# Where the products with v stand in the step of an attention kernel, and GpSimd's subtraction in four parts

## The chip, the cores and the metric

The kernel runs on one core of a Trainium2 chip. The metric is the device time of one execution in microseconds (us); three executions of the kernel before are known, and one more that was recorded by the hardware profiler. The engines are written as the profile writes them: PE is TensorE (PEld its weight loads), DVE VectorE, ACT ScalarE, POOL GpSimd, and SP the engine whose queue issues most of the DMAs.

## The reference, cut to what matters

Attention with a learned position bias for 4 batches and 8 heads, 576 positions and 64 channels, and behind it a feed-forward layer on the 2304 tokens:

```python
scores = scale * np.matmul(q, k.transpose(0, 1, 3, 2))
psi_rel = np.log1p(np.abs(pos[:, None] - pos[None, :]))
psi_i = np.log1p(np.maximum(pos[:, None], 1.0))
h = np.maximum((psi_rel / psi_i)[..., None] @ w1 + b1, 0.0)
scores = scores + (h @ w2).transpose(2, 0, 1)[None]
attn = np.exp(scores - np.max(scores, axis=-1, keepdims=True))
attn = attn / (np.sum(attn, axis=-1, keepdims=True) + 1e-09)
x = np.matmul(attn, v).transpose(0, 2, 1, 3).reshape(2304, 512)
h = x @ w_in
sp = np.where(h > 20.0, h, np.log1p(np.exp(np.minimum(h, 20.0))))
out = (h * np.tanh(sp)) @ w_out
```

The weights of the layer come as 64-bit floats.

## The kernel before, in words

The program has three stages: the position bias is computed and written to DRAM (to about 57 us of the profile), then the attention (to about 358 us), then the feed-forward layer. The change touches the attention alone.

**Pairs and steps.** The 32 products of batch and head are worked on as 16 pairs of heads (`i`, four pairs of heads `hp` with four batches `b` each). A pair has five steps, in the order 0, 1, 4, 2, 3 of its row chunks `c`; their places are `x` = 0 to 4, and steps are numbered `n` = 5i + x. The order of instructions on every engine is the order in which the code is written (there is no scheduler), and each engine works in order. One call of `step(n)` writes:

- `scores(n)` (L218): 16 matmuls of 128x288 columns into two units of PSUM (`s`; two buffers). The row of q is multiplied as a rounded part (`qkhi`) and a remainder (`qlo`). Then `add_bias` on DVE (L234), which writes `pt` and the row's maximum `m`, and `exps(n, 0)` on ACT (L249).
- `transposes(n - 2)`: PE turns the exponentials of the step before the last one, 128x128 at a time (L283, L286; for chunk 4 L296, L300), and ACT copies them to `main` and `tail` (L284, L290, L297, L301). PSUM has three buffers `tp` for it. The reciprocals' turn at x = 1 (L289) goes through a copy on DVE (`rt`, L264).
- `exps(n, 1)`, `ahead(n)` with the loads to come, and `split(n)` with pieces of work for later.
- `pv_duo`: the products with v. Chunks 0 and 1 of a pair form group 0, chunks 4, 2 and 3 group 1. A group has five products (`k` = 0 to 4) of two heads, that share 128x64 halves of the array, and gather in one PSUM tile `o`, of which there is one buffer. When k = 4 is done, DVE copies it to `x` (L327) and SP stores that to DRAM.

A group's five products are spread over steps: group 0 at x = 4 (two), x = 0 (two) and x = 1 (one), group 1 at x = 2 (three) and x = 3 (two).

**What comes ahead.** At x = 0 of pair i `ahead` issues the loads for pair i + 1: `qkhi` (1216 KB, L170) on POOL's queue, and `rawqk` (two halves of 304 KB, L161 and L162) and v on SP's. There are two buffers of `qkhi` and one of `rawqk`. `split` has POOL compute the remainders: `split_k` (L175) and `split_q` (L180) subtract the rounded values from the raw ones, 64x1216 elements each. They run for pair i + 1 while PE is on pair i; `rawqk` comes free when split_q has read it. In every fourth pair SP's queue also carries the bias of the next two heads, 2.6 MB in pieces, ahead of the next `rawqk`. SP's queue carries the weights of the layer too (L105), which DVE turns into 32-bit floats in pieces during all steps: L119, L122, L124 and L126, 32 weight tiles of 128x512.

For chunk 4, `exps` ends with a small copy inside `pt` on POOL (128x64, L252), which the transposes of chunk 4 need.

Of the kernel before, what the change touches and what calls it, by code (L numbers as in the profile page):

```python
# [7 lines left out]
F32 = mybir.dt.float32  # L8
# [3 lines left out]
ALU = mybir.AluOpType  # L12
# [3 lines left out]
B, H, S, D, C = 4, 8, 576, 64, 32  # L16
# [5 lines left out]
QW = 1216  # L22
# [24 lines left out]
def kernel(ctx: ExitStack, tc, qk, v, wb, w2, w_in, w_out, psia, psi4, rinv, eye, out):  # L47
    nc = tc.nc
    pe, dve, act, pool, sp = nc.tensor, nc.vector, nc.scalar, nc.gpsimd, nc.sync
# [58 lines left out]
    def conv_weights(on_act):  # L108

        job, w = w64.pop(0)
        late = order.index(job) >= EARLY
        c = (ring if late else convp).tile([P, 512], F32, name="w32")
        cu = c.bitcast(U32)
        if on_act:
            act.mul(c, w.bitcast(F32)[:, :, 1], 2.0 ** -112)
        else:
            dve.tensor_scalar(c, w.bitcast(F32)[:, :, 1], 2.0 ** -112, None, op0=ALU.mult)  # L119

        def parts():
            dve.tensor_scalar(w[:, :, 0], w[:, :, 0], 29, None, op0=ALU.logical_shift_right)  # L122
            yield False
            dve.scalar_tensor_tensor(cu, cu, 3, w[:, :, 0], op0=ALU.logical_shift_left, op1=ALU.bitwise_or)  # L124
            yield False
            dve.scalar_tensor_tensor(cu, w[:, :, 1], 0x80000000, cu, op0=ALU.bitwise_and, op1=ALU.bitwise_or)  # L126
            w32.append((job, c))
            yield True
        return parts()
# [23 lines left out]
    qk_raw, qk_hi, q_lo, v_t, bias_t = {}, {}, {}, {}, {}  # L153
# [16 lines left out]
        pool.dma_start(out=hi, in_=qk[b, hp])  # L170
        qk_hi[i] = hi

    def split_k(i):
        kl = qk_hi[i][64:128, QW:]
        (pool if i else dve).tensor_tensor(kl, qk_raw[i][64:128], kl.bitcast(F32), op=ALU.subtract)  # L175

    def split_q(i):

        lo = q_los[i % 2]
        (pool if i else dve).tensor_tensor(lo[0:64], qk_raw.pop(i)[0:64], qk_hi[i][0:64, :QW].bitcast(F32), op=ALU.subtract)  # L180
        q_lo[i] = lo

    def load_bias(hp, c):
# [12 lines left out]
    NPAIR = B * HP  # L196
    steps = [(i, c) for i in range(NPAIR) for c in ORDER]
    NS = len(steps)
    pt_t, live, o_t, sums, rc = {}, {}, {}, {}, {}
# [39 lines left out]
    def exps(n, u):  # L239

        i, c = steps[n]
        if u == 1 and c == 4:
            return
        if i not in sums:
            sums[i] = st.tile([P, 9], F32, name="sums", bufs=3)
        pt, m = live[n]
        ps = pt[:, u * S:(u + 1) * S]
        k = 4 * u + c if c < 4 else 8
        act.activation(ps, ps, AF.Exp, bias=m[:, u:u + 1], scale=-1.0, accum_out=sums[i][:, k:k + 1])  # L249
        if c == 4:  # L250

            pool.tensor_copy(pt[:, S:640], pt[:, 512:S])  # L252

    def reciprocals(i):

# [5 lines left out]
    def store_reciprocals(i, r, tp):  # L261
        hp, b = divmod(i, B)
        rt = xs.tile([9, P], F32, name="rt", bufs=1)
        dve.tensor_copy(rt, tp[0:9, P:2 * P])  # L264
        sp.dma_start(out=r_d[b][hp], in_=rt)

    def transposes(n):
        i, c = steps[n]
        pt, m = live.pop(n)
        grp = 0 if c < 2 else 1  # L270
        if (i, grp) not in pt_t:
            w = 256 if grp == 0 else 320
            main = ptp.tile([P, 2, 4, w], F32, name=f"main{grp}")
            tail = ptp.tile([P, 256 if grp == 0 else 384], F32, name=f"tail{grp}")
            pt_t[i, grp] = (main, tail)
        main, tail = pt_t[i, grp]
        if c < 4:
            off = c * P if grp == 0 else 64 + (c - 2) * P
            for h in range(2):
                tp = t_ps.tile([P, 512], F32, name="tp")  # L280
                for k in range(4):
                    c0 = h * 640 + k * P
                    pe.transpose(tp[:, k * P:(k + 1) * P], pt[:, c0:c0 + P], ident)  # L283
                act.copy(main[:, h, :, off:off + P], tp.rearrange("p (k q) -> p k q", k=4))  # L284
            tp = t_ps.tile([P, 512], F32, name="tp")
            pe.transpose(tp[:, :P], pt[:, 512:640], ident)  # L286
            r = rc.pop(n, None)
            if r is not None:
                pe.transpose(tp[0:9, P:2 * P], r, ident)  # L289
            act.copy(tail[:, off:off + P], tp[:, :P])  # L290
            if r is not None:
                store_reciprocals(i, r, tp)
        else:
            tp = t_ps.tile([P, 512], F32, name="tp")
            for k in range(4):
                pe.transpose(tp[:, k * P:(k + 1) * P], pt[:, k * P:(k + 1) * P], ident)  # L296
            act.copy(main[:, :, :, 0:64].rearrange("p h k q -> p k h q"),  # L297
                     tp.rearrange("p (k h q) -> p k h q", k=4, h=2))
            tp = t_ps.tile([P, 512], F32, name="tp")
            pe.transpose(tp[:, :P], pt[:, 512:640], ident)  # L300
            act.copy(tail[:, 0:64], tp[:, 0:64])  # L301
            act.copy(tail[:, 320:384], tp[:, 64:128])

    def pv_duo(i, grp, k):
        hp, b = divmod(i, B)
        main, tail = pt_t[i, grp]
        vt = v_t[i]
        w = 256 if grp == 0 else 320
        if k == 0:
            o_t[0] = o_ps.tile([P, 512], F32, name="o")  # L310
        o = o_t[0]
        kw = dict(skip_group_check=True)
        if k < 4:
            for h in range(2):
                pe.matmul(o[h * 64:h * 64 + 64, :w], vt[:, h, k, :], main[:, h, k, :],  # L315
                          start=(k == 0), stop=False, **kw)
            return
        if grp == 0:
            for h in range(2):
                pe.matmul(o[h * 64:h * 64 + 64, :w], vt[:, h, 4, :], tail, start=False, stop=True, **kw)  # L320
        else:
            pe.matmul(o[0:64, :w], vt[:, 0, 4, :], tail[:, 0:320], start=False, stop=True, **kw)
            pe.matmul(o[64:128, 64:320], vt[:, 1, 4, :], tail[:, 64:320], start=False, stop=True, **kw)
            pe.matmul(o[64:128, 0:64], vt[:, 1, 4, :], tail[:, 320:384], start=False, stop=True, **kw)
        del pt_t[i, grp]
        x = xs.tile([P, 320], F32, name="x")
        dve.tensor_copy(x[:, :w], o[:, :w])  # L327
        if grp == 0:
            sp.dma_start(out=x_d[b][:, hp, 0:256], in_=x[:, :256])
        else:  # L330
            sp.dma_start(out=x_d[b][:, hp, 256:512], in_=x[:, 64:320])
            sp.dma_start(out=x_d[b][:, hp, 512:576], in_=x[:, 0:64])

    LAG = 2
# [47 lines left out]
    def split(n):  # L382

        i, x = divmod(n, 5)
        if (x == 1 or n == 3) and i + 1 < NPAIR:
            split_k(i + 1)
        if x == 3 and i + 1 < NPAIR:
            split_q(i + 1)

        for _ in range((2, 2, 2, 1, 2)[x]):  # L390
            if not conv and w64:
                conv.append(conv_weights(x == 2))
            elif conv and next(conv[0]):
                conv.clear()
                load_weights()
                if w32[0][0] in order[:EARLY]:
                    split_weights(pool)

    def step(n):
        i, x = divmod(n, 5)  # L400
        late = n == 4

        def begin():
            if n < NS:
                scores(n)
                add_bias(n)
                exps(n, 0)

        def end():
            if n < NS:  # L410
                exps(n, 1)
                ahead(n)
            if 0 <= n - 1 < NS and (n - 1) % 5 == 4:
                rc[n - 1] = reciprocals((n - 1) // 5)
            if n < NS:
                split(n)


        if not late:
            begin()  # L420
        for k in {3: (0, 1)}.get(n, (n - LAG,)):
            if 0 <= k < NS:
                transposes(k)
        if not late:
            end()

        if late:
            for k in range(5):
                pv_duo(0, 0, k)
        for j, grp, ks in {4: ((i, 0, (0, 1)),), 0: ((i - 1, 0, (2, 3)),), 1: ((i - 1, 0, (4,)),),  # L430
                           2: ((i - 1, 1, (0, 1, 2)),), 3: ((i - 1, 1, (3, 4)),)}[x]:
            if 0 <= j < NPAIR and (j, grp) != (0, 0):
                for k in ks:
                    pv_duo(j, grp, k)
        if late:
            begin()
            end()

# [34 lines left out]
    for idx, t in enumerate(ts):  # L475
        spent["a"] += 1.0 + (1.9 if idx in SOFT_AT else 0.0)
        spent["v"] += (1.7 if idx in SOFT_AT else 0.0) + (1.4 if idx in (9, 12) else 0.0)
        n = reach(t)[2]
# [36 lines left out]
    for idx in range(NB + 2):  # L515
        if idx < NB:
            t = ts[idx]
            make_h(idx + 2)
            n = reach(t)[2]
# [32 lines left out]
    for n in range(len(SOFT_AT), NS):  # L552
        step(n)
# [103 lines left out]
    hidden(*units[0])  # L657
    step(NS + 1)
    step(NS + 2)
    step(NS + 3)  # L660
    left_scope.close()

    wq = sbuf("wq")
# [82 lines left out]
```

## Time and profile before

| | |
|---|---|
| median of three executions | 769.67 us (769.43 to 774.86) |
| profiled execution, its own time | 776.47 us |
| its span, first to last instruction | 774.7 us |
| attention stage within it | about 57 to 358 us |
| granted clock of PE, mean | 0.977 |

The profiled execution is 6.8 us above the median and 1.6 us above the highest of the three. All rows below come from it. A row of a timeline has the start in us from the span's start, the busy time in us, the engine, the line, the operation, what is written and read, the shape and the count; a bracket at its end gives the engine's idle time before it and what ended that.

### The profile page before, as it was taken

How to read it: one execution, taken by the hardware profiler on the slowest of the kernel's cores; microseconds unless marked ns; L12 is line 12 of the kernel's file. 1: busy time of each engine (PE TensorE's matmuls, PEld its weight loads, DVE VectorE, ACT ScalarE, POOL GpSimd, SP SyncE). 2: the span in 40 equal slices, each digit the busy share in tenths (PEclk: the TensorE clock that was granted, in tenths of full speed). 3: DMA queues.
4: the chain of work that ended last, by engine and by line, in shares of the span. 5: the costliest groups of instructions: out<-in, count | busy, mean ns of one | idle time of the engine just before them, and what ended most of it. 6: DMA issues, size and time to landing. Idle time of an engine off the chain costs nothing.

```text
span 774.7 us, 11579 instructions
## 1 busy us (share of the span) xinstructions
PE 723.3 (93%) x4160; PEld 553.0 (71%) x4160; DVE 525.1 (68%) x1047; ACT 459.5 (59%) x982; POOL 110.9 (14%) x76
## 2 busy tenths in 40 slices
PE   6688989899988998979999999999999999999997
PEld 3226667676766676756888888888987888888886
DVE  7974788678857876744977856656557566665554
ACT  6986777677756776746766644444444554444443
POOL 1003443333332334350000000000000000000000
PEclk9989999999989999989999999999999999999999
DMA  8988469876975697820400003000410500010001
GB/s 280 297 282 278 121 207 316 211 238 189 320 213 165 200 320 227 252 52 16 117 1 2 0 20 90 0 1 1 129 35 1 136 0 1 1 55 1 1 0 55
DMA packets 45610, 93.60 MB, mean 121 GB/s; under 512 B 13408, under 2 KB 22256, under 8 KB 43504
## 3 DMA queue, kind: packets, MB, share of 16 engines
q1 hardware_dynamic: 42672, 72.70, 32.0%
q0 software_dynamic: 2304, 19.92, 7.8%
q8 instruction: 33, 0.54, 0.3%
q10 hardware_dynamic: 576, 0.22, 0.1%
q14 instruction: 25, 0.20, 0.1%
HBM read 72.43 MB, written 20.40 MB: 120 GB/s over the span
## 4 chain that ended last, share of the span: by engine, by line
PE 57%; DMA 16%; DVE 8%; ACT 5%; POOL 3%; issue 2%; SPq 2%; DVEq 0%; POOLq 0%; ACTq 0%
PE y L631 24%; PE h L593 24%; DMA rawqk<-in_qk_dram 4%; PE s L218 3%; PE o L315 3%; DMA bias<-bias_d 3%; DMA w<-in_w_out_dram 3%; DVE pt L234 2%; PE tp L283 2%; POOL qkhi L175 1%; ACT pt L249 1%; DMA w<-in_w_in_dram 1%; DMA vt<-in_v_dram 1%; ACT main L284 1%; DMA qkhi<-in_qk_dram 1%
## 5 line engine op out<-in xcount | busy, mean ns | idle before, releaser
L249 ACT ACTIVATE pt<-pt,m 128x576 f32<-128x576 f32 x144 | 112.8, 784 | 90.5 <-DVE m L234 90.5
L234 DVE CUSTOM_DVE_ANT_0 pt<-s,bias 128x576 f32<-128x576 f32 x144 | 103.8, 752 | 38.9 <-PE s L218 38.1
L631 PE MATMUL y<-who,ghi 128*128 128x512 f32 x288 | 113.8, 395 | 0.2 <-ACT ghi L615 0.2
L631 PE MATMUL y<-who,glo 128*128 128x512 f32 x288 | 113.9, 396 | 0.0
L631 PE MATMUL y<-wlo,ghi 128*128 128x512 f32 x288 | 113.7, 395 | 0.0
L615 ACT CAST ghi<-e 128x512 fp32r<-128x512 f32 x72 | 44.7, 621 | 89.9 <-DVE e L611 89.8
L315 PE MATMUL o<-main,vt 128*64 128x320 f32 (+1 forms) x512 | 79.8, 436 | 8.1 <-DVE x L327 8.0
L598 ACT ACTIVATE e<-h 128x512 f32<-128x512 f32 x72 | 42.9, 598 | 71.4 <-PE h L593 71.4
L218 PE MATMUL s<-qkhi 128*128 128x288 f32 x320 | 79.2, 330 | 3.9 <-issue 2.7
L599 DVE TENSOR_SCALAR e<-e 128x512 f32<-128x512 f32 x72 | 30.7, 426 | 76.2 <-ACT e L598 76.2
L593 PE MATMUL h<-xhi,whi 128*128 128x512 f32 (+1 forms) x320 | 81.0, 373 | 0.8 <-ACT xhi L575 0.7
L593 PE MATMUL h<-xlo,whi 128*128 128x512 f32 (+1 forms) x320 | 80.4, 372 | 0.9 <-DVE xlo L577 0.8
L593 PE MATMUL h<-xhi,wli 128*128 128x512 f32 (+1 forms) x320 | 80.0, 371 | 0.0
L616 DVE TENSOR_TENSOR glo<-e,ghi 128x512 fp32r<-128x512 f32 x72 | 49.7, 690 | 43.8 <-ACT ghi L615 43.8
L218 PE MATMUL s<-qkhi,qlo 128*128 128x288 f32 x320 | 71.0, 304 | 6.3 <-POOL qlo L180 6.3
L218 PEld LDWEIGHTS s<-qkhi 128*128 128x128 f32 x320 | 51.5, 195 | 32.5 <-issue 22.0
L283 PE MATMUL tp<-ident,pt 128*128 128x128 f32 x512 | 69.6, 281 | 1.0 <-ACT main L284 0.9
L284 ACT COPY main<-tp 128x512 f32<-128x512 f32 x128 | 67.7, 578 | 0.7 <-PE tp L283 0.5
L593 PEld LDWEIGHTS h<-xhi,whi 128*128 128x128 f32 x320 | 57.2, 188 | 14.1 <-ACT xhi L575 2.1
L593 PEld LDWEIGHTS h<-xlo,whi 128*128 128x128 f32 x320 | 56.8, 188 | 12.9 <-DVE xlo L577 1.7
L593 PEld LDWEIGHTS h<-xhi,wli 128*128 128x128 f32 x320 | 56.8, 188 | 11.3
L631 PEld LDWEIGHTS y<-who,glo 128*128 128x128 f32 x288 | 54.1, 188 | 13.7 <-DVE glo L616 0.9
(75 smaller groups left out, 1160.6 us busy)
## 6 DMA issues: line engine op xcount, KB each, us to landing
qkhi<-in_qk_dram POOLq DMA_DIRECT2D x16, 1216.0 KB, 7.7
bias_d<-bt SPq DMA_DIRECT2D x36, 295.5 KB
rawqk<-in_qk_dram SPq DMA_DIRECT2D x32, 304.0 KB
w<-in_w_in_dram SPq DMA_DIRECT2D x16, 512.0 KB
w<-in_w_out_dram SPq DMA_DIRECT2D x16, 512.0 KB
vt<-in_v_dram SPq DMA_DIRECT2D x16, 320.0 KB
bias<-bias_d SPq DMA_DIRECT2D x16, 288.0 KB
out_dram<-w SPq DMA_DIRECT2D x17, 256.0 KB
```

What stands on the lines that cost most here:

```text
L218: pe.matmul(s[:, j, :SH], stat[:, q0:q0 + P], hi[:, QW + kc + j * SH:QW + kc + (j + 1) * SH], start=(k == 0), stop=(k == len(todo) - 1))
L234: dve.tensor_tensor_reduce(out=halves(pt[:, sl]), in0=s[:, :, :SH], in1=halves(bt[:, sl]), scale=-0.125, scalar=BIG, op0=ALU.add, op1=ALU. ...
L249: act.activation(ps, ps, AF.Exp, bias=m[:, u:u + 1], scale=-1.0, accum_out=sums[i][:, k:k + 1])
L283: pe.transpose(tp[:, k * P:(k + 1) * P], pt[:, c0:c0 + P], ident)
L284: act.copy(main[:, h, :, off:off + P], tp.rearrange("p (k q) -> p k q", k=4))
L315: pe.matmul(o[h * 64:h * 64 + 64, :w], vt[:, h, k, :], main[:, h, k, :], start=(k == 0), stop=False, **kw)
L593: pe.matmul(h[:, u * n:(u + 1) * n], w["i", g4, d][:, r * P:(r + 1) * P], x[:, d, :n], start=(k == 0), stop=(k == 11))
L598: act.activation(e, h, AF.Exp)
L599: dve.tensor_scalar(e, e, E20, None, op0=ALU.min)
L615: act.copy(ghi, e)
L616: dve.tensor_tensor(glo, e, ghi.bitcast(F32), op=ALU.subtract)
L631: pe.matmul(ys[blk][t], g[:, c0:c0 + P], w, start=(f == 0 and k == 0), stop=(f == NFC - 1 and k == 2))
```

## The change

The five products of a group are issued in one step: group 0 at x = 4, group 1 at x = 2 of the next pair. They stand between the step's scores and its transposes (n = 4 keeps an order of its own). The copy of `o` and the store of `x` come at the end of the same step. `split_k` and `split_q` of pairs 1 to 15 are written as four subtractions of 64x304 each; those of K in steps x = 1 and 2, those of q in x = 3 and 4 (for pair 1 all eight at n = 3). The small copy for chunk 4 goes from POOL to ACT.

```diff
+    QPART = QW // 4
+    def split_k(i, parts=range(4)):
+        for r in parts if i else (slice(0, QW),):
+            r = r if i == 0 else slice(r * QPART, (r + 1) * QPART)
+            kl = qk_hi[i][64:128, QW:][:, r]
+            (pool if i else dve).tensor_tensor(kl, qk_raw[i][64:128, r], kl.bitcast(F32), op=ALU.subtract)
...
-            pool.tensor_copy(pt[:, S:640], pt[:, 512:S])
+            act.copy(pt[:, S:640], pt[:, 512:S])
...
         del pt_t[i, grp]
+
+    def store_x(i, grp):
...
-        if (x == 1 or n == 3) and i + 1 < NPAIR:
-            split_k(i + 1)
-        if x == 3 and i + 1 < NPAIR:
-            split_q(i + 1)
+        if i + 1 < NPAIR:
+            if n == 3:
+                split_k(1)
+                split_q(1)
+            elif i and x == 1:
+                split_k(i + 1, (0, 1))
...
+        pv = [(j, grp) for at_x, j, grp in ((4, i, 0), (2, i - 1, 1)) if x == at_x and 0 <= j < NPAIR]
...
+        if late:
+            turn()
+            products()
+        begin()
         if not late:
-            begin()
-        for k in {3: (0, 1)}.get(n, (n - LAG,)):
-            if 0 <= k < NS:
-                transposes(k)
-        if not late:
-            end()
...
+            products()
+            turn()
+        end()
+        for j, grp in pv:
+            store_x(j, grp)
...
-    step(NS + 3)
```

On PE before, from the end of the scores at x = 4 of a pair over x = 0 of the next (`main_1096` belongs to group 0; the count is of k and heads):

```order
L218 MATMUL s<-qkhi,qlo_117 128x288 x2
L296 MATMUL tp<-ident,pt_1092 128x128 x4
L300 MATMUL tp<-ident,pt_1092 128x128
L315 MATMUL o<-main_1096,vt 64x256 x4
L218 MATMUL s<-qkhi 128x288 x2
L218 MATMUL s<-qkhi,qlo_116 128x288 x2
L218 MATMUL s<-qkhi 128x288 x2
L218 MATMUL s<-qkhi,qlo_116 128x288 x2
L283 MATMUL tp<-ident,pt 128x128 x8
L286 MATMUL tp<-ident,pt 128x128
L315 MATMUL o<-main_1096,vt 64x256 x4
L218 MATMUL s<-qkhi 128x288 x2
```

Two products stand behind the transposes of either step. The same place now:

```order
L225 MATMUL s<-qkhi,qlo_117 128x288 x2
L322 MATMUL o<-main_1115,vt 64x256 x8
L327 MATMUL o<-tail_1116,vt 64x256 x2
L303 MATMUL tp<-ident,pt_1099 128x128 x4
L307 MATMUL tp<-ident,pt_1099 128x128
L225 MATMUL s<-qkhi 128x288 x2
L225 MATMUL s<-qkhi,qlo_116 128x288 x2
L225 MATMUL s<-qkhi 128x288 x2
L225 MATMUL s<-qkhi,qlo_116 128x288 x2
L290 MATMUL tp<-ident,pt 128x128 x8
L293 MATMUL tp<-ident,pt 128x128
L225 MATMUL s<-qkhi 128x288 x2
```

All ten have moved between the scores and the transposes of x = 4, and x = 0 holds scores and transposes alone.

On POOL before, one round for a pair (K, the small copy, q, the next load):

```order
L175 TENSOR_TENSOR qkhi<-rawqk,qkhi 64x1216
L252 COPY pt_1535<-pt_1535 128x64
L180 TENSOR_TENSOR qlo_116<-rawqk,qkhi 64x1216
L170 DMA qkhi<-in_qk_dram 128x2432
L175 TENSOR_TENSOR qkhi<-rawqk,qkhi 64x1216
```

And now:

```order
L180 TENSOR_TENSOR qkhi<-rawqk,qkhi 64x304 x4
L187 TENSOR_TENSOR qlo_116<-rawqk,qkhi 64x304 x4
L170 DMA qkhi<-in_qk_dram 128x2432
L180 TENSOR_TENSOR qkhi<-rawqk,qkhi 64x304 x4
L187 TENSOR_TENSOR qlo_117<-rawqk,qkhi 64x304 x4
```

Nothing stands between K and q any more, and each is four instructions.

On SP before, ahead of the load of `rawqk`, from x = 3 of a pair to x = 0 of the next:

```order
L331 DMA x_d_80<-x 128x256
L332 DMA x_d_80<-x 128x64
L105 DMA w_2077<-in_w_in_dram 128x1024
L161 DMA rawqk<-in_qk_dram 64x1216
L162 DMA rawqk<-in_qk_dram 64x1216
```

And now, from x = 2:

```order
L343 DMA x_d_81<-x 128x256
L344 DMA x_d_81<-x 128x64
L105 DMA w_2342<-in_w_in_dram 128x1024
L341 DMA x_d_82<-x 128x256
L161 DMA rawqk<-in_qk_dram 64x1216
L162 DMA rawqk<-in_qk_dram 64x1216
```

The store of group 0 has come to stand right before the load of `rawqk`; it stood at x = 1 of the next pair, behind it.

## Rows read from the trace of the kernel before

**Rows 1.** Whom PE waited for from 56 to 358 us: us in total, times, longest us.

```profile
PE tp L300 <- POOL pt L252: 8.8, 5, 3.2
PE o L315 <- DVE x L327: 7.1, 10, 2.7
PE s L218 <- POOL qlo L180: 6.3, 5, 3.8
...
PE s L218 <- DVE m L234: 1.3, 2, 0.9
PE tp L283 <- ACT main L284: 0.9, 2, 0.6
```

**Rows 2.** PE's timeline: a step without products (from 74.03 us) and one with a group's last product (from 94.89 us).

```profile
74.03 0.51 PE L218 MATMUL s<-qkhi 128*128 128x288 f32 x2
...
75.17 1.03 PE L283 MATMUL tp<-ident,pt 128*128 128x128 f32 x8
...
76.18 0.51 PE L218 MATMUL s<-qkhi 128*128 128x288 f32 x2
...
94.89 1.04 PE L283 MATMUL tp<-ident,pt 128*128 128x128 f32 x8
...
96.08 0.65 PE L320 MATMUL o<-tail,vt 128*64 128x256 f32 x4
96.66 0.53 PE L218 MATMUL s<-qkhi 128*128 128x288 f32 x2
```

**Rows 3.** PE's timeline over one pair, from x = 0 to the next x = 0: its first scores, products of eight matmuls and the scores behind them, the only wait in the pair, the next pair's first scores.

```profile
243.31 0.53 PE L218 MATMUL s<-qkhi 128*128 128x288 f32 x2
...
245.54 1.08 PE L315 MATMUL o<-main,vt 128*64 128x256 f32 x8
246.56 0.53 PE L218 MATMUL s<-qkhi 128*128 128x288 f32 x2
...
252.27 1.83 PE L315 MATMUL o<-main,vt 128*64 128x320 f32 x12 [0.48 <-DVE x L327]
...
260.32 0.53 PE L218 MATMUL s<-qkhi 128*128 128x288 f32 x2
```

**Rows 4.** The timeline of all engines at 231 us, where POOL and DVE meet.

```profile
231.24 0.41 DVE L122 TENSOR_SCALAR w<-w 128x512 uint32<-128x512 uint32 x1
...
231.56 2.74 POOL L175 TENSOR_TENSOR qkhi<-rawqk,qkhi 64x1216 fp32r<-64x1216 f32 x1 [9.28 <-DMA rawqk<-in_qk_dram]
...
231.69 3.17 DVE L124 SCALAR_TENSOR_TENSOR w<-w,w 128x512 uint32<-128x512 uint32 x1
...
235.24 1.84 PE L315 MATMUL o<-main,vt 128*64 128x320 f32 x12 [2.69 <-DVE x L327]
...
235.79 0.68 DVE L126 SCALAR_TENSOR_TENSOR w<-w,w 128x512 uint32<-128x512 uint32 x1
```

**Rows 5.** DVE's groups by shape from 58 to 358 us: count, busy us, mean ns of one, idle us before them.

```profile
L126 DVE SCALAR_TENSOR_TENSOR w<-w,w 128x512 uint32<-128x512 uint32 x32 | 28.7, 896 | 0.5
L124 DVE SCALAR_TENSOR_TENSOR w<-w,w 128x512 uint32<-128x512 uint32 x32 | 28.6, 895 | 0.5
L122 DVE TENSOR_SCALAR w<-w 128x512 uint32<-128x512 uint32 x32 | 24.2, 755 | 0.8 <-DMA w<-in_w_out_dram 0.8
```

**Rows 6.** POOL's timeline: ends of two rounds of K, small copy and q, the begin of the next round, and two products of 128x512 back to back.

```profile
219.00 2.76 POOL L180 TENSOR_TENSOR qlo<-rawqk,qkhi 64x1216 fp32r<-64x1216 f32 x1
...
236.90 0.24 POOL L252 COPY pt<-pt 128x64 f32<-128x64 f32 x1 [2.59 <-ACT pt L249]
...
257.64 0.59 POOL L252 COPY pt<-pt 128x64 f32<-128x64 f32 x1
258.19 2.79 POOL L180 TENSOR_TENSOR qlo<-rawqk,qkhi 64x1216 fp32r<-64x1216 f32 x1
...
271.66 2.79 POOL L175 TENSOR_TENSOR qkhi<-rawqk,qkhi 64x1216 fp32r<-64x1216 f32 x1 [10.17 <-DMA rawqk<-in_qk_dram]
...
339.62 2.49 POOL L380 TENSOR_TENSOR xraw<-xraw,xr 128x512 f32<-128x512 f32 x2 [2.46 <-DMA xr<-r_d]
```

**Rows 7.** The timeline of all engines in the pair behind a load of bias: the load of `rawqk` leaves SP's queue, K's subtraction begins, PE waits for the small copy behind it.

```profile
129.55 0.57 SPq L161 DMA_DIRECT2D rawqk<-in_qk_dram  x1
...
141.72 2.75 POOL L175 TENSOR_TENSOR qkhi<-rawqk,qkhi 64x1216 fp32r<-64x1216 f32 x1 [13.55 <-DMA rawqk<-in_qk_dram]
...
144.91 0.33 PE L300 MATMUL tp<-ident,pt 128*128 128x128 f32 x1 [2.05 <-POOL pt L252]
```

**Rows 8.** The timeline of all engines at x = 1 of the pair of rows 3 (its scores on PE begin at 246.56 us).

```profile
247.39 0.76 DVE L234 CUSTOM_DVE_ANT_0 pt<-s,bias 128x576 f32<-128x576 f32 x1 [0.86 <-PE s L218]
...
248.25 0.77 ACT L249 ACTIVATE pt<-pt,m 128x576 f32<-128x576 f32 x1 [0.49 <-DVE m L234]
...
249.02 1.05 ACT L284 COPY main<-tp 128x512 f32<-128x512 f32 x2
...
249.96 0.28 ACT L290 COPY tail<-tp 128x128 f32<-128x128 f32 x1
```

**Rows 9.** The stretches of the attention in which PE's clock was granted at half (the second of six, and the sum of all): us, busy us and counts by engine, granted clock, DMA share, GB/s.

```profile
83.82:87.24 3.42, 3.42 (x15) 2.31 (x16) 0.73 (x3) 3.42 (x10) 2.36 (x2) 0.50 0.49 156
...
sum 27.31, PE 25.50 PEld 18.73 DVE 18.76 ACT 18.33 POOL 13.51; mean PE 4.25 PEld 3.12 DVE 3.13 ACT 3.06 POOL 2.25
```

**Rows 10.** DVE's waits from 26 to 60 us, the end of the bias stage: us in total, times, longest us.

```profile
DVE pt L234 <- PE s L218: 5.2, 1, 5.2
```

More of the change, by code (lines that the diff above doesn't have):

```diff
@@ L171, in load_hi, with split_q @@
         qk_hi[i] = hi
[L173 to L177, printed above, removed]
+    QPART = QW // 4
[4 more added lines that the diff above has]
+            (pool if i else dve).tensor_tensor(kl, qk_raw[i][64:128, r], kl.bitcast(F32), op=ALU.subtract)
+    def split_q(i, parts=range(4)):
         lo = q_los[i % 2]
-        (pool if i else dve).tensor_tensor(lo[0:64], qk_raw.pop(i)[0:64], qk_hi[i][0:64, :QW].bitcast(F32), op=ALU.subtract)
+        for r in parts if i else (slice(0, QW),):
+            r = r if i == 0 else slice(r * QPART, (r + 1) * QPART)
+            (pool if i else dve).tensor_tensor(lo[0:64, r], qk_raw[i][0:64, r], qk_hi[i][0:64, r].bitcast(F32), op=ALU.subtract)
         q_lo[i] = lo
@@ L325, in pv_duo @@
         del pt_t[i, grp]
+    def store_x(i, grp):
+        hp, b = divmod(i, B)
+        w = 256 if grp == 0 else 320
+        o = o_t[0]
         x = xs.tile([P, 320], F32, name="x")
@@ L384, in split @@
         i, x = divmod(n, 5)
-        if (x == 1 or n == 3) and i + 1 < NPAIR:
-            split_k(i + 1)
-        if x == 3 and i + 1 < NPAIR:
-            split_q(i + 1)
+        if i + 1 < NPAIR:
[4 more added lines that the diff above has]
+                split_k(i + 1, (0, 1))
+            elif i and x == 2:
+                split_k(i + 1, (2, 3))
+            elif i and x >= 3:
+                split_q(i + 1, ((0, 1), (2, 3))[x - 3])
         for _ in range((2, 2, 2, 1, 2)[x]):
@@ L416, in end, with products, turn @@
                 split(n)
-        if not late:
-            begin()
-        for k in {3: (0, 1)}.get(n, (n - LAG,)):
-            if 0 <= k < NS:
-                transposes(k)
-        if not late:
-            end()
[L427 to L437, printed above, removed]
+        pv = [(j, grp) for at_x, j, grp in ((4, i, 0), (2, i - 1, 1)) if x == at_x and 0 <= j < NPAIR]
+        def products():
+            for j, grp in pv:
+                for k in range(5):
+                    pv_duo(j, grp, k)
+        def turn():
+            for k in {3: (0, 1)}.get(n, (n - LAG,)):
+                if 0 <= k < NS:
+                    transposes(k)
+        if late:
+            turn()
+            products()
+        begin()
+        if not late:
+            products()
+            turn()
+        end()
+        for j, grp in pv:
+            store_x(j, grp)
     bc = bsbuf("bc")
```

## Prediction

> **What bounds the kernel now.** I read the waits of PE first. From 56 to 358 us PE is what the attention is made of, and three entries hold nearly all its losses: 8.8 us for POOL's small copy, 7.1 us for DVE's copy of `o`, 6.3 us for the remainder of q [rows 1]. What is to be seen is that none of the three is work of PE: each is a place where another engine, in its own order, stands behind something else.
>
> Then one quiet pair, to see PE's own price. From 243.31 to 260.32 us it takes 17.01 us, of which 0.48 is the wait for `o` [rows 3]. So 16.53 us are PE's work and what its changes of kind cost.
>
> Then the steps. A step without products takes 75.17 - 74.03 = 1.14 us of scores and 76.18 - 75.17 = 1.01 us of ten transposes. One with a group's last product takes 96.66 - 94.89 = 1.77 us from the transposes to the next scores [rows 2]. Eight product matmuls take 246.56 - 245.54 = 1.02 us [rows 3], four take 96.66 - 96.08 = 0.58 [rows 2], so one is 0.11 us and four are 0.44. The rest, 1.77 - 1.01 - 0.44 = 0.32 us, is what one visit to the products costs, whatever is done in it.
>
> Then DVE and POOL. At 231.69 us an L124 that should take about 0.68 us (L126 beside it, of the same kind, does) takes 3.17: it ends 0.56 us after POOL's K subtraction does. The copy of `o` stands behind it, and PE waits 2.69 us [rows 4]. Against 0.68 and 0.41 us unhindered [rows 4], the groups of DVE lose 32 x (0.896 - 0.68) = 6.9 us in L126, 6.9 in L124 and 32 x (0.755 - 0.41) = 11.0 in L122 [rows 5]: some 25 us of DVE's time, mostly hidden.
>
> Last, the loop that runs beside PE: q subtracted, `rawqk` free, the next load, K subtracted, q subtracted. From the end of q's subtraction to the begin of the next K it takes 231.56 - 221.76 = 9.8 us [rows 4, 6] or 271.66 - 260.98 = 10.7 us [rows 6]. With two subtractions of 2.76 and a copy this makes some 16.5 us, as long as PE's pair. Where bias was loaded it is longer: the load leaves SP at 129.55 us and K begins at 141.72 [rows 7]. There PE waits, whatever it does before.
>
> **The change, part by part.** *Visits to the products* fall from five to two a pair: 3 x 0.32 = 0.96 us less. This counts where PE sets the pace. Of the pairs 2 to 14 I leave out the bias pairs 3, 7 and 11 and the ones behind them, 4, 8 and 12, paced by DMA, and count pair 1: 8 pairs, -7.7 us. The price is measured for transposes to products to scores; the new order is scores to products to transposes. Bounds: nothing saved, or 0.96 in all 14, -13.4.
>
> *The wait for `o`.* The copy of `o` now has two or three steps of time before the next group needs the buffer, where it had none. The 7.1 us go: -7.1. At either end this is the surest term.
>
> *What is late next there.* The products now stand right behind the scores, so they need ACT's copies of the step before sooner. In rows 8, from the begin of the scores at 246.56 [rows 3], the first bias add comes at +0.83, the exponential at +1.69, the two `main` copies from +2.46 to +3.51, `tail` until +3.68. With no products in between PE would be there after 1.14 + 1.01 + 1.14 = 3.29 us [rows 2]. So PE waits 0.22 us at least at x = 4. At x = 2 it is more: two light steps come in a row, and the 0.86 us that DVE had idle before this add [rows 8] vanish with the 1.02 us of products of the step before. I take 0.5 there, 0.7 a pair, 8 pairs: +5.6. Bounds: 0, and 1.5 us a pair, where all of ACT's lateness falls on PE.
>
> *POOL's parts.* 64x1216 takes 2.74 us [rows 4], 128x512 2.49 / 2 = 1.25 back to back [rows 6]. The line through both has 0.16 us at zero columns and 2.1 ns a column, so 64x304 should take 0.80 us. Eight are 6.4 us against 2 x 2.76 plus a copy of 0.24 to 0.59 [rows 6], 5.8 to 6.1. The loop would then be 9.8 to 10.7 + 6.4 = 16.2 to 17.1 us. PE would like 17.01 - 0.48 - 0.96 + 0.7 = 16.27 us. The loop's middle, 16.65, is 0.4 above that: +3.2 in 8 pairs. Bounds: 0, and the third rival.
>
> *What the parts give.* Scores of x = 0 need q in pieces: the first unit its first quarter, the second its third. So the first unit can go 5 x 0.80 = 4.0 us after K begins, the second 7 x 0.80 = 5.6; before, both stood until about 5.9 (141.72 to 2.76 behind the copy's end at 144.86) [rows 7]. PE gains between 0.3 and 1.9 us in each place where it waits for `rawqk`. I take 1 in the three pairs behind a bias load, and 1 in the last, where the longest wait of 3.8 us is [rows 1]: -4.0.
>
> *DVE's losses.* A DVE operation can now be held for the rest of one part, 0.8 us, not 2.74. Most of the 25 us were hidden; what shows besides `o` is PE's 1.3 and 0.9 us behind `m` and ACT's copies [rows 1], of which I take 1.5: -1.5. The clock was at half from 83.82 to 87.24 us behind these two waits; if they go, 3.42 / 2 = 1.7 us go with it [rows 9]: -1.7.
> The row shows an operation of DVE held until POOL's whole instruction was over. The Trainium skill, SBUF — State Buffer, "Who interferes with whom", says that DVE and GpSimd share a pair of ports as an exclusive lock, which whoever starts first keeps for the whole instruction. By it four parts cut the hold to one part, as summed; but it works both ways, and each part can lose the lock to DVE, which is the third rival.
>
> *The small copy.* On POOL it stood behind K's subtraction, which waits for DMA; on ACT it stands behind the exponential that it needs. Of the five waits, two of about 0.66 us go: -1.3. The other three (2.05 us in rows 7, up to 3.2 in rows 1; 7.5 together) come in the pairs behind bias loads, where K begins late: PE runs on and meets the same delay at x = 0. I take nothing; bound: all 7.5. On ACT the copy costs 16 times about 0.25 us, hidden in its idle time (0.49 us before one exponential, rows 8); without that cover 4 us.
>
> *The store of x* now stands ahead of `rawqk`'s load on SP, and with it the wait for the products of x = 4 and DVE's copy. That copy follows the same pieces of conversion that held the weights' load ahead of `rawqk` before. I take 0; bound 0.8 us a pair (a copy and an issue), in the pairs that the loop sets, which is inside the loop's bounds.
>
> *The start and the end.* For pair 1 POOL no longer waits for the small copy, so its eight parts run in the bias stage and hold DVE there by up to 6.4 us. DVE finishes that stage 5.2 us early [rows 10]: +1.0. The drain has two visits fewer: -0.6.
>
> **The sum.** -7.7 - 7.1 + 5.6 + 3.2 - 4.0 - 1.5 - 1.7 - 1.3 + 1.0 - 0.6 = -14.1 us. The profiled execution would come to 776.5 - 14.1 = 762.4 us. It lies 6.8 us above the median of 769.67, and some of its waits may be missing in the others; I take the same 14.1 us off the median: **755.6 us**.
>
> **The rivals.** *1: the DMA pairs recover too.* If `rawqk` lands earlier because everything ahead of it on SP does, the 7.5 us of waits for the small copy go, and so does half of the half-clock time behind them, (27.31 - 3.42) / 4 = 6.0 us [rows 9]. For it: SP's bias loads are issued as DVE frees the tiles, so they follow PE's pace. Against: 12 us from issue to K is a queue of bytes, not of waits. 755.6 - 13.5 = 742 us.
>
> *2: the new wait eats the visits.* If PE waits 1.44 us a pair for ACT's copies, the sum of 0.96 and the old 0.48, the pair is as long as before: +5.9, and with nothing gained behind bias loads (+3) the time is 764.5 us. For it: PE's two light steps of 2.15 us each meet an ACT that needs 3.68 us from scores to `tail`. Against: the heavy steps let DVE and ACT catch up.
>
> *3: POOL's loop becomes the bound, and the kernel slower.* The place is POOL between K's first part and q's last. Each part that meets a conversion piece on DVE waits for it, 0.41 to 0.69 us. If four of eight do, the loop is 16.65 + 2.2 = 18.85 us: +2.2 in 8 pairs and in 3 behind bias loads, 24 us: 780 us. It decides from a round of 7.2 us on, 0.9 a part, where the loop passes the 17.0 us of today's pair. For it: the small copy took 0.59 us instead of 0.24 once [rows 6], so POOL is held too. Against: 2.74 to 2.80 for whole subtractions shows that it is seldom.
>
> *4: the parts don't do what they should.* If POOL goes from part to part with DVE still held, DVE loses up to 2.7 us as before, now behind `m`; without -3.2 and with one wait of 2 us more: 761 us. No row shows two POOL instructions with a DVE operation held between them.
>
> **How the numbers follow.** Forecast 0.46, rival 1 0.14, rival 2 0.20, rival 3 0.10, rival 4 0.10. One per cent of the median, 7.7 us, is about what the three runs can tell from no change: they reach 0.7% apart. Below 762.0 us lie the forecast, rival 1 and two thirds of rival 4: 0.67. Above 777.4 lies rival 3: 0.10. The rest, 0.23, is within. The range takes in rivals 2 and 4, the forecast with its bounds (the wait for ACT from 0 to 1.5 us a pair, visits up to -13.4) and all but the end of rival 1: 742 to 772 us.
>
> **What would show it.** PE's waits for the small copy and for `x` should be gone, those for `qlo` larger in the three pairs behind bias loads, and a new one for ACT's `main` should stand before the products, under 1 us. A part should take 0.8 us, a round of eight 6.4 to 7. No conversion piece on DVE should take over 1.6 us. A quiet pair should take 16.3 to 16.7 us. The forecast is wrong if a part takes over 0.9 us, or if the wait before the products passes 1.4 us.

## The result and the profile after

The changed kernel takes 782.38 us (781.1 to 783.32) against 772.22 of the kernel before (769.43 to 774.86): a ratio of 1.0114, with an interval from 1.0072 to 1.0157. The forecast was 755.6 us, faster by 1.8%; the measured time is 10.2 us above the kernel before and 10 us above the range. The profiled execution takes 782.27 us (span 780.1), 5.8 us more than the profiled one of before; that one lies 4.3 us above its median, so the profiles show little more than half of the loss.

Whom PE waits for in the changed kernel from 56 to 362 us (us in total, times, longest; answers to [rows 1]):

```profile
PE s L225 <- POOL qlo L187: 12.9, 16, 1.4
PE o L322 <- ACT main L291: 7.4, 7, 3.7
PE s L225 <- issue: 3.9, 1, 3.9
PE s L225 <- DVE m L241: 2.8, 6, 1.0
PE s L225 <- POOL qkhi L180: 2.4, 3, 1.6
```

The waits for the small copy and for `x`, 15.9 us before, are gone, as forecast. PE now waits for POOL's parts, 19 times in 15 pairs.

A quiet pair on PE (answers to [rows 3]): first scores, the first of two visits to products, the next pair's first scores.

```profile
247.13 0.51 PE L225 MATMUL s<-qkhi 128*128 128x288 f32 x2
...
252.82 2.58 PE L322 MATMUL o<-main,vt 128*64 128x320 f32 x15 [0.21 <-ACT main L291]
...
263.43 0.51 PE L225 MATMUL s<-qkhi 128*128 128x288 f32 x2
```

It takes 16.30 us, where 16.27 was forecast. What PE does by itself became shorter, though by less than was forecast (see below). The other side is POOL. Its groups from 58 to 358 us, and then DVE's conversions (answers to [rows 5]):

```profile
L187 POOL TENSOR_TENSOR qlo<-rawqk,qkhi 64x304 fp32r<-64x304 f32 x56 | 51.6, 949 | 1.0
L180 POOL TENSOR_TENSOR qkhi<-rawqk,qkhi 64x304 fp32r<-64x304 f32 x56 | 49.2, 904 | 143.6 <-DMA rawqk<-in_qk_dram 135.9 <-DMA qkhi<-in_qk_dram 7.5
```

```profile
L126 DVE SCALAR_TENSOR_TENSOR w<-w,w 128x512 uint32<-128x512 uint32 x32 | 26.5, 827 | 0.5
L124 DVE SCALAR_TENSOR_TENSOR w<-w,w 128x512 uint32<-128x512 uint32 x32 | 24.3, 760 | 0.5
L122 DVE TENSOR_SCALAR w<-w 128x512 uint32<-128x512 uint32 x32 | 17.3, 540 | 4.3 <-DMA w<-in_w_out_dram 4.3
```

DVE got back 13 us of the 25 that these three groups lost in meetings, 32 x (0.069 + 0.135 + 0.215). POOL lost: a part takes 0.90 (K) and 0.95 us (q) in the mean, not 0.80.

The timeline of all engines at one such place (answers to [rows 4]):

```profile
163.28 3.37 POOL L180 TENSOR_TENSOR qkhi<-rawqk,qkhi 64x304 fp32r<-64x304 f32 x4 [11.19 <-DMA rawqk<-in_qk_dram]
164.90 0.66 ACT L117 ACTIVATE w<-w 128x512 f32<-128x512 f32 x1 [4.08 <-DMA w<-in_w_out_dram]
164.91 1.05 DVE L122 TENSOR_SCALAR w<-w 128x512 uint32<-128x512 uint32 x1 [2.79 <-DMA w<-in_w_out_dram]
...
166.72 2.06 POOL L187 TENSOR_TENSOR qlo<-rawqk,qkhi 64x304 fp32r<-64x304 f32 x2
...
166.84 2.03 PE L322 MATMUL o<-main,vt 128*64 128x256 f32 x7 [3.66 <-ACT main L291]
...
168.14 1.20 DVE L126 SCALAR_TENSOR_TENSOR w<-w,w 128x512 uint32<-128x512 uint32 x1
```

Both engines hold each other up here: L122 takes 1.05 us where 0.42 is its median, two parts of q 2.06 where 1.63 is the value without a hold. And PE waits 3.66 us for ACT, which itself stands 4.08 us at L117 for the weights' DMA.

The chain of waits of the changed kernel over one pair (start, us, what) shows what sets the pace:

```profile
132.86 11.29 DMA rawqk<-in_qk_dram
...
145.09 2.58 POOL qkhi L180 x3
...
147.74 3.06 POOL qlo L187 x3
...
152.90 0.45 SPq L164
...
153.44 11.44 DMA w<-in_w_out_dram
...
164.90 0.66 ACT w L117
...
166.84 3.37 PE o L322 x15
...
170.90 0.43 DVE x L339
...
171.35 0.32 SPq L341
...
171.78 0.47 SPq L161
```

There is little of PE in it: load, K, q, the loads behind q on SP's queue, the weights' conversion, the products, the store of `x`, the next load.

**The loop in numbers.** From the timelines of POOL and SP I take, for the 13 rounds between K of pair 2 and K of pair 15: from K's begin to q's end; from there to the issue of `rawqk`'s load, which I call the slack, since the buffer is free and SP isn't ready; from the issue to the next K. All are sums in us.

| kernel | K to q | slack | load to K | time / time before |
|---|---|---|---|---|
| before | 87.0 | 27.0 | 136.1 | 1 |
| after | 98.3 | 10.1 | 141.6 | 1.0114 |
| e1_whole | 79.9 | 40.0 | 117.0 | 0.9884 |
| e2_pair1_late | 99.3 | 10.8 | 141.9 | 1.0056 |
| e3_parts_only | 103.1 | 4.1 | 146.8 | 1.0093 |
| e4_products_only | 83.0 | 34.0 | 119.9 | 0.9895 |
| e5_whole_late | 79.8 | 38.0 | 118.8 | 0.9886 |
| e6_halves | 87.0 | 19.5 | 136.1 | 0.9995 |

In the changed kernel six of the 13 loads leave within 0.03 us of q's end, before three, in e1 none. Against the kernel before, the slack shrank by 17 us; 11.3 of it went into longer rounds and 5.5 into longer loads, so the 13 rounds take 250 us in both. With the products' new place and whole subtractions (e1, e4) they take 237: the parts cost the 13 us that the new place gains. A round and a load take (98.3 + 141.6) / 13 = 18.5 us in the changed kernel, against 16.3 of PE's quiet pair: the loop sets the pace.

In e1 and e4 the load leaves some 3 us a round behind q's end. The buffer is free then, but SP stands at the store of `x`: in all 13 rounds of either it is the last issue ahead of the load, which follows 0.1 us behind it. So there the load waits for PE's products of x = 4. The same holds for the seven loads of the changed kernel that don't leave at q's end. (In e1 a load takes 9.0 us in the mean, in the changed kernel 10.9. In e1 it leaves 3 us behind `qkhi`'s, so that the two probably share less of their time; this wasn't tested.)

**The bias stage.** Timelines of POOL and of DVE at its end in the changed kernel, then of DVE in the kernel before:

```profile
34.47 3.47 POOL L180 TENSOR_TENSOR qkhi<-rawqk,qkhi 64x304 fp32r<-64x304 f32 x4 [30.37 <-DMA rawqk<-in_qk_dram]
38.02 3.43 POOL L187 TENSOR_TENSOR qlo<-rawqk,qkhi 64x304 fp32r<-64x304 f32 x4
```

```profile
35.84 7.00 DVE L518 TENSOR_SCALAR ht<-at,bb 128x304 f32<-128x304 f32 x11
```

```profile
35.89 6.86 DVE L496 TENSOR_SCALAR ht<-at,bb 128x304 f32<-128x304 f32 x22
```

While the eight parts of pair 1 run on POOL (34.47 to 41.45 us), DVE does 11 instructions in the time of 22. The first scores of pair 1 begin at 74.18 us instead of 70.62 (the changed kernel first):

```profile
74.18 0.82 PE L225 MATMUL s<-qkhi 128*128 128x288 f32 x2 [3.91 <-issue]
```

```profile
70.62 0.58 PE L218 MATMUL s<-qkhi 128*128 128x288 f32 x1 [2.66 <-issue]
```

That is 3.6 of the 5.4 us by which the span grew. At K of pair 2 the changed kernel is 5.3 us behind (83.11 against 77.80), and as the 13 rounds take as long in both, it stays there. So between these two profiles the parts show as a gain that failed to come, and the growth itself lies ahead of pair 2.

### The profile page after: what moved, and what is told of

Read it like the earlier page. It is cut to its first block, busy times and chain, and to the rows that moved or that the text cites. A ratio compares the mean times of both kernels' runs of the same rounds, so it can differ in the third digit from the quotient of the medians.

```text
span 780.1 us, 11588 instructions
## 1 busy us (share of the span) xinstructions
PE 724.4 (93%) x4160; PEld 568.3 (73%) x4160; DVE 516.3 (66%) x1047; ACT 464.9 (60%) x998; POOL 129.4 (17%) x150
## 4 chain that ended last, share of the span: by engine, by line
PE 57%; DMA 19%; POOL 5%; ACT 5%; DVE 4%; SPq 2%; issue 1%; DVEq 0%; POOLq 0%; ACTq 0%
PE h L615 24%; PE y L653 24%; DMA rawqk<-in_qk_dram 6%; DMA w<-in_w_out_dram 4%; DMA bias<-bias_d 4%; PE o L322 4%; POOL qkhi L180 2%; POOL qlo L187 2%; PE s L225 2%; ACT pt L256 2%; PE tp L290 1%; DVE pt L241 1%; DMA xr<-r_d 1%; DMA qkhi<-in_qk_dram 1%; DMA xlo<-r_d 1%
## 5 line engine op out<-in xcount | busy, mean ns | idle before, releaser
L322 PE MATMUL o<-main,vt 128*64 128x320 f32 (+1 forms) x512 | 82.6, 423 | 8.3 <-ACT main L291 7.4
L225 PE MATMUL s<-qkhi 128*128 128x288 f32 x320 | 77.2, 323 | 9.2 <-issue 3.9
L225 PE MATMUL s<-qkhi,qlo 128*128 128x288 f32 x320 | 72.2, 308 | 12.9 <-POOL qlo L187 12.9
L180 POOL TENSOR_TENSOR qkhi<-rawqk,qkhi 64x304 fp32r<-64x304 f32 x60 | 52.7, 903 | 174.0 <-DMA rawqk<-in_qk_dram 166.3
L290 PE MATMUL tp<-ident,pt 128*128 128x128 f32 x512 | 71.8, 286 | 1.0 <-ACT main L291 0.9
L322 PEld LDWEIGHTS o<-main,vt 128*64 128x64 f32 x512 | 44.9, 140 | 34.1 <-ACT main L291 17.2
```

What stands on the lines that cost most here:

```text
L180: (pool if i else dve).tensor_tensor(kl, qk_raw[i][64:128, r], kl.bitcast(F32), op=ALU.subtract)
L225: pe.matmul(s[:, j, :SH], stat[:, q0:q0 + P], hi[:, QW + kc + j * SH:QW + kc + (j + 1) * SH], start=(k == 0), stop=(k == len(todo) - 1))
```

## The experiments

Theory A: the parts are the loss, through the loop of load, K and q that sets the pace. Theory B: the products' new place is. Each ratio is to executions of the kernel before that were taken beside the run; their medians lie between 772.0 and 774.2 us.

**e1_whole**

```diff
-    def split_k(i, parts=range(4)):   (and split_q)
+    def split_k(i):                   64x1216 at x = 1; split_q at x = 3
```

> The changed kernel with the subtractions of K and q whole again (64x1216, K at x = 1, q at x = 3, pair 1 both at n = 3); the products' new place and the small copy on ACT stay. Theory A (the parts are the loss: between pairs 2 and 15 POOL's rounds grew by 11.2 us, from 87.1 to 98.3, and gave back the 11.4 us that the loads got shorter): a round takes 5.5 to 5.7 us, quiet pairs take 16.3 us, and the time is 770 us, 766 to 774. Theory B (the products' new place is the loss: a wait of PE for ACT's copies and the store of x ahead of rawqk): rounds get shorter but PE's wait for main stays at 7 us, and the time is 780 us, 777 to 783.

766.51 us, ratio 0.9884 (0.9849 to 0.9919). A round takes 79.9 / 13 = 6.1 us, more than the 5.5 to 5.7 expected. PE's wait for `main` before the products fell to 1.2 us. DVE lost 36 us in meetings (the time over the median of its kind, of each instruction that took over 0.1 us more), against 18 in the changed kernel, and yet e1 is 2.3% faster than that. Theory B falls.

**e4_products_only**

```diff
 (the kernel before, with)
+            products()      # between scores and transposes
+            turn()
+        for j, grp in pv:
+            store_x(j, grp)
```

> The kernel before with the products' new place and the store of x at the end of the step alone; subtractions whole and small copy on POOL as before. Theory A: the visits saved in the quiet pairs (0.7 us in some six, 4 us) and the waits for x (7 us) come off where the loop doesn't set the pace, half of 11 us: 766 us, 762 to 770. Theory B: the new place is the loss, 776 to 782 us.

766.24 us, 0.9895 (0.9852 to 0.9939): the new place alone gains 1.05%.

**e3_parts_only**

```diff
 (the kernel before, with)
-            split_k(i + 1)
+                split_k(i + 1, (0, 1))   and so on, 64x304 each
```

> The kernel before with the four-part subtractions alone, in the steps that the change gives them; products and small copy as before. Theory A: a round of eight with the copy takes 7.3 to 8 us instead of 6.2, 1.1 to 1.8 us in each of 13 rounds, against 1 us gained where PE waits for q in pieces: 772 + 10 = 782 us, 776 to 787. Theory B: the parts are neutral or a small gain: 769 to 774 us.

781.91 us, 1.0093 (1.006 to 1.0126): the parts alone lose nearly 1%. The two don't add up: the parts cost 0.9% on the old kernel and 2.3% behind the products' new place (e1 against the changed kernel), probably since on the old kernel PE's own pair of 17.0 us hides part of the longer loop.

**e6_halves**

```diff
-    QPART = QW // 4
+    QPART = QW // 2
```

> The changed kernel with two subtractions of 64x608 instead of four of 64x304, one in each of the same steps. It asks what a part costs. If each instruction of POOL has a fixed price and a chance of being held at its start, a round of four lies a third of the way from the whole ones (mean of rounds 6.15 us) to the quarters (7.56): 6.6 us, and the time at 771 us, 768 to 775. If the loss is that POOL can be held at all (one hold is enough), a round takes 7.2 us or more and the time is 778 to 783 us.

770.67 us, 0.9995 (0.9954 to 1.0036), a mean round of 87.0 / 13 = 6.7 us, the round and the time of the kernel before. The price goes with the number of instructions. Counted as held where an instruction takes over 0.1 us more than the median of its kind, 33 of the 112 parts were held in the changed kernel, 18 of 56 halves here: 29 and 32%, by 0.32 us each. In e1 8 of 28 whole ones were, also 29%: a chance at each start. The rest is the fixed price: a whole one takes 2.78 us, four parts back to back 4 x 0.80 = 3.20.

**e2_pair1_late**

```diff
-            act.copy(pt[:, S:640], pt[:, 512:S])
+            (act if i else pool: the same copy)
```

> The changed kernel with one edit: the small copy of pair 0 alone goes back to POOL, so that POOL's queue holds the eight parts of pair 1 until after the bias stage, as it did before the change. Theory A (in the bias stage the parts hold DVE and cost 3.6 us up to the first scores of pair 1): these scores begin at 70.6 us instead of 74.2, the time is 779 us, 777.5 to 780.5. Rival: the 3.6 us come from the load of the first weights, which DVE waits for 9.2 us there, and not from POOL: the scores stay at 73 to 74 us, the time at 782 us.

777.79 us, 1.0056 (1.0022 to 1.0089), first scores of pair 1:

```profile
68.88 0.82 PE L225 MATMUL s<-qkhi 128*128 128x288 f32 x2 [3.15 <-issue]
```

That is 5.3 us earlier than in the changed kernel, while DVE's wait for the weights is much the same (8.3 us, 9.2 there): the rival falls. With the small copy on ACT, nothing held POOL back in the bias stage any more. By the two ratios this is 0.6 of the 1.14% that the change lost, with intervals nearly as wide.

**e5_whole_late**, both edits at once:

> The changed kernel with whole subtractions (as e1_whole) and pair 0's small copy on POOL (as e2_pair1_late): both undone at once. Theory A, where the two losses add up: 766.5 - 4 = 762 us, 759 to 766, the first scores of pair 1 at 69 to 71 us and a mean round of 6.1 us from pair 3 on. Rival (the pairs behind are paced by loads that start at fixed times, so an earlier begin is given back): 766 us, 764 to 769.

763.86 us, 0.9886 (0.9826 to 0.9946). The first scores of pair 1 begin at 70.7 us, 3.0 earlier than in e1, and the attention ends 3.0 earlier, but the ratio is e1's: the interval of some 4.6 us doesn't tell 3 us.

**e9_raw2_parts**

```diff
-    rawp = rsbuf("raw", 1, side="right")
+    rawp = rsbuf("raw", 2, side="right")
```

> The changed kernel with one edit: two buffers of rawqk instead of one, so that the next load no longer waits for the end of q's subtraction; the eight parts stay. Theory A (the loop of load, K, q sets the pace, and the parts cost time only through it): the loop is cut open, from the end of q to the next K it takes 6 to 8 us instead of 11.7, with a round of 7.3 this makes 14 to 15 us, under PE's 16.3; quiet pairs take 16.3 us, and the time is 755 us, 745 to 766. Rival (the loads are paced by the bytes of all queues, not by their begin; or POOL's hold reaches PE through DVE): K begins no earlier, 776 to 783 us.

769.93 us, 0.9967 (0.9929 to 1.0006): 12 us off the changed kernel with all parts in place, but half of what was expected. Whom POOL waited for from 76 to 345 us, the changed kernel first and then this one:

```profile
POOL qkhi L180 <- DMA rawqk<-in_qk_dram: 135.9, 13, 13.5
```

```profile
POOL qkhi L180 <- DMA qkhi<-in_qk_dram: 82.2, 9, 11.0
POOL qkhi L180 <- DMA rawqk<-in_qk_dram: 45.6, 5, 11.5
```

The loop has a second link: `qkhi`'s load stands on POOL's own queue behind q's parts. With one wait cut, the other holds.

**e10_raw2_whole_late**

> e5_whole_late with two buffers of rawqk. Theory A: with the loop open, whole subtractions and parts differ by less than 4 us apart from the 4 us of the bias stage: e9_raw2_parts less 4 us, with 0 to 4 us more off for DVE's and POOL's meetings; 750 us, 740 to 760. Rival (a whole subtraction that holds DVE for 2.8 us shows once PE sets the pace): slower than e9_raw2_parts. If the loads are paced by bytes: 760 to 765 us, as e5_whole_late.

763.56 us, 0.9895 (0.9853 to 0.9937), as e5_whole_late. With whole subtractions the second buffer changes nothing, and theory A's 750 us failed. The table has the reason: in e5 all but one of the 13 loads already leave 1.8 to 4.9 us behind q's end, 38.0 us in all, so it is seldom the buffer that they wait for. The time is also what the rival "paced by bytes" forecast; e12 below, with the same bytes in 752 us, rules that out.

**e13_conv_on_dve**

```diff
-                conv.append(conv_weights(x == 2))
+                conv.append(conv_weights(False))
```

> The changed kernel with one edit: the first step of every weight's conversion runs on DVE; before, one in three ran on ACT (L117) and stood there for the weights' DMA, up to 4.1 us, with the exponentials and the copies to main behind it. Theory C (the 7.4 us that PE waits for main are this wait for weights, whose load stands on SP behind rawqk's and so behind q): the waits for main fall below 2 us, the time to 776 us, 773 to 779. Rival (DVE stands in the same place, and the bias adds behind it): PE waits as long for m or main as before, 780 to 784 us. Theory D (ACT is late by its own work): the waits for main stay at 6 to 8 us, 781 to 784 us.

781.54 us, 1.0124 (1.0097 to 1.0151). PE's waits:

```profile
PE s L225 <- DVE m L241: 10.5, 11, 3.4
PE s L225 <- POOL qlo L187: 10.4, 13, 1.4
...
PE o L322 <- ACT main L291: 1.3, 4, 0.6
```

The wait went over to the engine that stands for the weights: `main` 1.3 us instead of 7.4, `m` 10.5 instead of 2.8. Theory D falls, and the rival holds. What PE waits for there is late loads.

**e11_loads_ahead_whole** and **e12_loads_ahead_parts**, with two buffers of `rawqk` and

```diff
-        if x == 0 and i + 1 < NPAIR:
-            load_hi(i + 1)
-            load_raw(i + 1)
+        if x == 3 and i + 2 < NPAIR:
+            load_raw(i + 2)
+        if x == 4 and i + 2 < NPAIR:
+            load_hi(i + 2)
```

> e10_raw2_whole_late with the loads issued earlier: rawqk and v of pair i + 2 at x = 3 of pair i, qkhi of pair i + 2 at x = 4 of pair i (before: both for i + 1 at x = 0 of pair i). In e9_raw2_parts K began 0.1 us after qkhi landed in most pairs, in e10_raw2_whole_late after rawqk, which stood on SP behind the stores of x: with one wait of the loop cut, another link took its place. Theory A (the loop in all its links sets the pace outside the quiet pairs): with rawqk there long before, from the end of q to the next K it takes 7 to 9 us, the loop 13 to 15, all pairs but those that carry bias take 16.3 to 17 us: 750 us, 742 to 757. Rival (bytes: all queues together can't bring a pair's loads in 16.3 us): no gap shorter than 9 us, 760 to 766 us.

> The same loads, with the eight parts of the changed kernel (and pair 0's small copy on POOL). Theory A: the round of 7.3 to 7.7 us and 7 to 9 us of loads make 14.5 to 16.5, at PE's pair: the parts cost 0 to 6 us against e11_loads_ahead_whole, not 14 as between e5_whole_late and e2_pair1_late; 753 us, 744 to 762. Rival (the parts cost time by something else than the loop, such as DVE's or PE's waits for each part): 12 us or more above e11_loads_ahead_whole.

e12 takes 752.11 us, 0.9738 (0.9709 to 0.9767): it beats both kernels. Early loads alone don't do it: e11, which differs in the parts alone, takes 778.59 us, 1.0092 (1.0056 to 1.0129), outside the ranges of its theory and its rival. I had expected e11 to be the faster. PE's waits in e11, the first of them in e12, and one of e11's in its timeline:

```profile
PE s L219 <- DVE m L235: 15.2, 11, 3.2
PE tp L287 <- ACT main L288: 10.7, 15, 0.9
```

```profile
PE s L225 <- DVE m L241: 1.6, 6, 0.3
```

```profile
136.72 2.81 POOL L181 TENSOR_TENSOR qlo<-rawqk,qkhi 64x1216 fp32r<-64x1216 f32 x1
...
136.85 2.97 DVE L122 TENSOR_SCALAR w<-w 128x512 uint32<-128x512 uint32 x1
...
139.73 0.74 DVE L235 CUSTOM_DVE_ANT_0 pt<-s,bias 128x576 f32<-128x576 f32 x1
...
140.54 0.53 PE L219 MATMUL s<-qkhi 128*128 128x288 f32 x2 [3.24 <-DVE m L235]
```

A conversion piece is held for q's whole subtraction, the bias add stands behind it, and PE, which has two buffers of scores, stops for 3.24 us. From 72 to 345 us PE's clock was granted at 0.94 in the mean, against 0.99 in e12; five stretches at half speed begin within 1 us of the end of such a wait. An estimate from these means: against full speed the clock cost 0.06 x 273 = 16 us in e11 and 3 in e12, which is half of the 26 us between the two. In e12 PE waits 1.6 us for `m`. DVE's holds don't vanish there, they get shorter: 38.5 us in all against 46.9, the longest 1.9 against 2.6 (over the median of the kind). So the parts pay once the loop is off PE's back; before that, the same edit costs time.

**e14_loads_ahead_spread**, e12 with the products in their old place:

> e12_loads_ahead_parts with the products and the stores of x back in their old places (a group's five products spread over three or two steps, behind the transposes; v's load moved from x = 3 to x = 4, since its buffer comes free later); two buffers of rawqk, early loads, parts and the small copy as in e12. What is the products' new place worth where PE sets the pace? Theory A: what the quiet pairs show (0.44 us of PE and the wait of 0.48 for x, in 14 pairs, 13 us) shows in full: 764 us, 760 to 769, a ratio of 0.990 to the kernel before, with 5 us or more of waits for x back. Rival (the early loads alone make the gain, the products' place is hidden): 750 to 756 us, a ratio of 0.974.

759.46 us, 0.9824 (0.9777 to 0.9872). The waits for `x` are back, in nearly every pair:

```profile
PE o L328 <- DVE x L340: 19.8, 14, 2.0
```

The products' new place is worth some 0.9% here too, less than these 19.8 us; part of them goes into the pairs behind bias loads, which take 18.2 to 18.8 us in e12 against 17.1 to 18.1 here.

## Why the prediction was wrong

**The step that failed is POOL's parts**, the term of the loop. I set a loop of 16.65 us against PE's 16.27, added 0.4 us in 8 pairs, and left the pairs behind bias loads out as "paced by DMA". In the mean of all 13 rounds, those behind bias loads included, the loop measured 18.45, and 19.2 with the slack. Of the 1.8 us that were missing, 1.2 are the round: priced at 8 x 0.80 = 6.4, it took 98.3 / 13 = 7.6. Of these 1.2, 0.75 are holds (33 of 112 parts, 0.32 us each); in the first two rounds pieces of weights (L137, 1.3 and 1.6 us) stand between the parts too. The other 0.6 are the load: from q's end to K I had taken 9.8 and 10.7 us, two of the shorter ways, while the load alone took 141.6 / 13 = 10.9. PE's gains count only down to the loop's length. The kernel before had a loop of (87.0 + 136.1) / 13 = 17.2 us without slack, just above PE's own 17.0, and the prediction lowered the one and not the other; e1 and e4 show what the same PE gains are worth, 1.1%, while the rounds stay short. Both of the prediction's own signs of being wrong came true: a part of 0.93 us, and a wait before the products of 3.7.

**Rival 3 is what happened**, with its place (POOL between K's first part and q's last) and its point (a round of 7.2 us, 0.9 a part; measured 7.6 and 0.93). I had given it 0.10, because whole subtractions were seldom held. That row doesn't carry the reason: a whole subtraction starts once, parts start four times, and 29% of starts are held. That its price of 780 us came so near is partly luck: it had four of eight parts held for 2.2 us a round, where 2.4 of eight were, for 0.75, and some 4 us of the 782 belong to the bias stage.

**Visits to the products** saved 0.44 us in the quiet pair (16.53 to 16.30 - 0.21 = 16.09), not 0.96, and the new wait for ACT is 0.21 there, not 0.7. The two errors cancel, and that 16.27 came out is luck.

**The wait for `o`** and **the small copy**: the waits went as forecast, and what they gave went into the loop. As the prediction said of the pairs behind bias loads, PE met the delay again at x = 0.

**What the parts give** (-4.0): wrong in sign. PE's waits for the remainder of q grew from 6.3 to 12.9 us, and e3 shows the parts alone to cost 0.9%. The quarter that the second unit of scores needs was to be there 5.6 us behind K's begin; from pair 4 to pair 14 it came 5.7 to 6.8 us behind it, mostly later than the whole of q before (5.84 to 6.3 us in most rounds).

**DVE's losses**: the mechanism is right here, and no conversion took over 1.61 us. The gain didn't reach PE: e1 has the longer holds and is faster. The place where it does is e12 against e11.

**ACT**: up to 3.7 us stand before the products, but behind the weights' DMA, not behind ACT's own work. These loads stand behind `rawqk` on SP, and so behind q's end. The prediction followed SP's queue ahead of `rawqk` and not behind it.

**The bias stage** (+1.0): 3.6 in the trace up to the first scores of pair 1, because DVE's instructions there were held one after the other; e2 shows it.

**The store of `x`** (0): in e1 and e4 every load of `rawqk` stands behind it, by 40.0 and 34.0 us in all. What an earlier load would give there with nothing else changed wasn't tried; e12 has the load ahead of the store, together with other edits.

## What to carry to other kernels

Before an edit is priced, follow the closed loop over buffers (free, load, compute, free) through all pairs and take its mean, not its best: if it is longer than the busiest engine's own work, savings on that engine are worth little, and each microsecond on the loop counts in every round. Cutting an operation into parts trades the hold of the neighbour for holds of its own and a fixed price for each part; whether that pays depends on which of the two engines the pace hangs on, and the answer here changed sign when the loads were issued earlier. After a link of a loop is cut, look for the next one (`rawqk`, then `qkhi`), and before a buffer is added, look whether the load waits for the buffer at all or for an issue ahead of it on its queue.

## What the runs showed of the hardware

A DVE instruction can be held over several of POOL's. In e12, from the issue of a DMA on POOL over two parts:

```profile
156.72 0.57 POOL L170 DMA_DIRECT2D qkhi<-in_qk_dram  x1 [2.49 <-PE s L225]
...
157.04 2.46 DVE L124 SCALAR_TENSOR_TENSOR w<-w,w 128x512 uint32<-128x512 uint32 x1
157.31 1.63 POOL L187 TENSOR_TENSOR qlo<-rawqk,qkhi 64x304 fp32r<-64x304 f32 x2
```

L124 starts ahead of both parts and ends 0.56 us behind the second: that is rival 4, in these places. It is no single case. Of the 13 DVE instructions of e12 from 58 to 358 us that took over 1.2 us more than the median of their kind, 11 start while POOL issues this load and end 0.29 to 0.56 us behind the two parts that follow; the other two span two instructions of POOL without such an issue. In the changed kernel one instruction was held for that long.

The Trainium skill, SBUF — State Buffer, "Who interferes with whom", says that whichever issues first gets the shared pair for the whole instruction. The meeting at 164.90 us in the changed kernel agrees (L122 takes 0.63 us more than its median and ends 0.29 us behind the part of K that was running); the rows above show more, an instruction of DVE passed over by the next one of POOL.

DVE's bias add, which reads scores from PSUM and one operand from SBUF, was never held in the changed kernel: 140 instructions took between 0.735 and 0.759 us.
